# Scores of two query blocks in one run of matmuls, from the thirteenth visit on

## The chip, the cores and the metric

The kernel runs on one core of a Trainium2 chip. The metric is the device time of one execution in microseconds. Three runs of the kernel before gave 1351.29, 1351.37 and 1351.89 us; the median is 1351.37 us. One further execution was recorded by the profiler.

The core has five engines with a queue each: TensorE (PE: matmuls; PEld: its weight loads), VectorE (DVE), ScalarE (ACT), GpSimd (POOL) and SyncE (SP), which here only issues DMA transfers. TensorE writes its results into PSUM, eight banks of 512 fp32 words in each of 128 partitions.

## The reference

Attention with a threshold, and then an MLP with a squared relu:

```python
# q, k, v: (8, 8, 576, 64) fp32; tau = 0.02
scores = scale * np.matmul(q, k.transpose(0, 1, 3, 2))
thresh = np.max(scores, axis=-1, keepdims=True) - tau
scores = np.where(scores >= thresh, scores, -1000000000.0)
scores = scores - np.max(scores, axis=-1, keepdims=True)
attn = np.exp(scores)
attn = attn / (np.sum(attn, axis=-1, keepdims=True) + 1e-09)
attn_out = np.matmul(attn, v)
# (B, H, S, D) -> (B*S, H*D)
x = attn_out.transpose(0, 2, 1, 3).reshape(4608, 512)
h = x @ w_in            # 512 x 2048
r = np.maximum(h, 0.0)
out = (r * r) @ w_out   # 2048 x 512
```

Everything is fp32.

## The kernel before

**Visits and steps.** Two heads of one batch are handled together; this is a visit. A sequence of 576 rows is four blocks of 128 and a rest of 64. From the visit with number 12 on (the thirteenth, `paired`), visits go in pairs: an even visit has five steps, first the rests of both visits of the pair (`i == NBLK`), then blocks 0 to 3; an odd visit has blocks 0 to 3. So a pair has nine steps. One step is one block of queries of two heads against 576 keys.

**What a step does.** `scores` (line 254) issues four matmuls with 64 rows of the array each, one head in the upper and one in the lower half, two pieces of 288 columns per head. They go to the PSUM tiles `s0` and `s1`, two banks each. VectorE takes the maxima (line 276), ScalarE the exponents (line 292), VectorE drops what lies under the threshold and sums (`threshold`, line 304), GpSimd divides (`divide`, line 314). Then the weights must be turned, keys into partitions: in `turn_blocks` (line 394) VectorE transposes squares of 32 x 32 into a buffer `turned`, and in `place_blocks` (lines 406 and 411) SyncE's queue copies these with DMAs into `wT`. There are two halves of `turned`, taken in turn, and one `wT`.

**Values.** When all blocks of a visit lie in `wT`, `mix` (line 456) multiplies with v on TensorE, into two PSUM banks, and ScalarE copies the result into `xT`. Values come four steps after a visit's last scores (`mixes`, lag 4). As there is one `wT`, copies for the next visit wait until the values of the last have read it.

**The MLP beside it.** TensorE's time between is filled with pieces of the MLP, taken from the deque `waiting`. Each chunk of 256 tokens (from the third on) is done by a scheme with seven products in place of eight: `unit` (line 612, eight matmuls of 128 columns) makes hidden activations, `product` (line 713, in halves of four matmuls of 256 columns) the output. Sums that a unit or product needs are made by GpSimd and VectorE (line 543), evacuations by ScalarE and VectorE, squares by ScalarE and GpSimd. Units add up in PSUM, so a bank is kept over several pieces (`keep_bank`, `free`); there are four such banks, 4 to 7, and `values` sees to it that two of them are free before `mix`.

**What sets the order.** Each engine runs its instructions in the order in which the program issues them. The loop over steps writes that order out: scores, then what the last piece left to do (`after`), exponents, values where due, a quarter of the step's MLP pieces (`fill`), threshold and divide, a second quarter, `turn_blocks` of the step before and `place_blocks` of what is due (`place_at`), and the other quarters. `rate` sets how many pieces a step gets: it spreads what is waiting evenly over the steps to come, with an estimate of each piece (`PIECE_US`) and of values (`VALUES_US`).

## Time and profile before

| | us |
|---|---|
| median of three runs | 1351.37 |
| lowest and highest | 1351.29, 1351.89 |
| profiled execution, its own time | 1353.89 |
| its span, first to last instruction | 1352.1 |
| TensorE busy | 1314.7 (97%) |
| GpSimd busy | 972.6 (72%) |
| VectorE busy | 953.0 (70%) |
| ScalarE busy | 578.6 (43%) |
| mean granted clock of TensorE | 0.994 |

The profile is of one execution. Its rows give the line of the kernel, the engine, the operation, output and inputs by the program's names, the count, and then busy time and the mean of one in ns. "Idle before, releaser" names how long an engine stood before such an instruction and whose semaphore ended it; where the engine named had long been done, it was another, often a DMA. A timeline row has its start in the span, its length, and how many records it merges. An fp32 matmul leaves two records. Ends of matmuls are modelled, so distances are taken from start to start. The windows view has, for a stretch, the busy time of PE, PEld, DVE, ACT and POOL, then the granted clock, the share of the DMA engines and GB/s. SPq is SyncE's queue, where a row's length is that of issuing the DMA and not of the transfer.

Two stages can be told apart in the late part, from 282 us to 1200 us, where the paired visits' values lie: the steps with attention, and after them a tail of MLP alone until 1352 us.

### The profile page before, as it was taken

The numbers are of one execution on the slowest core, as the hardware profiler recorded it, in microseconds if no ns is written. First come the engines' busy times: TensorE is split into PE (matmuls) and PEld (weight loads), VectorE is DVE, ScalarE is ACT, GpSimd is POOL, SyncE is SP. The second block draws the span as 40 slices with busy tenths as digits, with TensorE's granted clock in tenths as the row PEclk, the third lists the DMA queues.
The fourth block names the chain that finished last, engine by engine and source line by source line (L and its number), as shares of the span: only waits on it lengthen the run. The fifth ranks groups of instructions, "written<-read, shape, count | busy, mean of one in ns | idle before, by whom it ended". The sixth has DMA issues, their size and how long they took to land.

```text
span 1352.1 us, 26266 instructions
## 1 busy us (share of the span) xinstructions
PE 1314.7 (97%) x9112; PEld 1062.1 (79%) x9112; DVE 953.0 (70%) x2026; ACT 578.6 (43%) x1309; POOL 972.6 (72%) x1229
## 2 busy tenths in 40 slices
PE   6899999999999999999999999999999999999998
PEld 5676556877787878787877887888878888889997
DVE  6877776977787878777867787878786777632231
ACT  4776674325353534343433444343434353422421
POOL 3679775797887979695969788868696867453451
PEclk7999999999999999999999999999999999999999
DMA  8764531445555656564545565545555554320000
GB/s 154 163 154 116 144 91 35 82 83 112 101 120 97 128 99 132 99 118 85 107 83 101 102 114 111 95 90 105 95 102 100 110 95 97 67 54 0 16 17 16
DMA packets 406356, 128.17 MB, mean 95 GB/s; under 512 B 390064, under 2 KB 394448, under 8 KB 406224
## 3 DMA queue, kind: packets, MB, share of 16 engines
q1 hardware_dynamic: 385632, 95.10, 38.1%
q0 software_dynamic: 18288, 31.11, 8.8%
q8 instruction: 73, 1.20, 0.4%
q10 hardware_dynamic: 2304, 0.29, 0.2%
q14 instruction: 59, 0.48, 0.1%
HBM read 50.59 MB, written 9.44 MB: 44 GB/s over the span
## 4 chain that ended last, share of the span: by engine, by line
PE 83%; DVE 5%; POOL 4%; ACT 3%; issue 2%; SPq 1%; DMA 1%; ACTq 0%; DVEq 0%; POOLq 0%
PE bank L612 28%; PE bank L713 26%; PE s L254 12%; PE bank L456 10%; PE bank L504 3%; PE bank L678 2%; PE bank L354 2%; POOL g L543 1%; DVE st L276 1%; DVE w L304 1%; ACT wT L355 1%; ACT w L292 1%; SPq L406 1%; POOL w L314 1%; DVE turned L394 1%
## 5 line engine op out<-in xcount | busy, mean ns | idle before, releaser
L276 DVE TENSOR_REDUCE st<-s 128x1 f32<-128x576 f32 x286 | 203.6, 750 | 139.9 <-PE s L254 139.5
L304 DVE SCALAR_TENSOR_TENSOR w<-s,st,w 128x576 f32<-128x576 f32 x269 | 208.9, 813 | 66.8 <-ACT w L292 66.5
L713 PE MATMUL bank<-wo,gsum 128*128 128x256 f32 x1088 | 245.9, 382 | 0.0
L314 POOL TENSOR_SCALAR w<-w,st 128x576 f32<-128x576 f32 x269 | 227.1, 854 | 22.9 <-DVE st L307 15.5
L713 PEld LDWEIGHTS bank<-wo,gsum 128*128 128x128 f32 x1088 | 204.0, 190 | 40.1 <-issue 10.8
L289 ACT ACTIVATE st<-st 128x2 f32<-128x2 f32 (+1 forms) x148 | 30.3, 205 | 397.1 <-DVE st L276 396.5
L713 PE MATMUL bank<-wo,g 128*128 128x256 f32 x816 | 186.4, 382 | 0.0
L394 DVE STREAM_TRANSPOSE turned<-w 128x512 f32<-128x512 f32 (+2 forms) x388 | 169.7, 491 | 21.5 <-DMA wT<-turned 19.9
L612 PE MATMUL bank<-xT,w_in_sb 128*128 128x128 f32 x1536 | 184.2, 276 | 0.6 <-ACT xT L439 0.6
L612 PEld LDWEIGHTS bank<-xT,w_in_sb 128*128 128x128 f32 x1536 | 177.8, 192 | 8.4 <-issue 4.9
L292 ACT ACTIVATE w<-s,st 128x576 f32<-128x576 f32 x269 | 183.3, 732 | 0.2 <-ACT st L290 0.2
L456 PE MATMUL bank<-wT,vs 128*64 128x128 f32 (+7 forms) x1700 | 170.8, 358 | 9.5 <-ACT wT L355 4.0
L254 PE MATMUL s<-kT,qT 64*128 64x288 f32 x1016 | 167.5, 433 | 11.0 <-DVE w L304 8.0
L713 PEld LDWEIGHTS bank<-wo,g 128*128 128x128 f32 x816 | 151.2, 190 | 28.0 <-issue 8.9
L312 POOL TENSOR_SCALAR st<-st 128x2 f32<-128x2 f32 (+1 forms) x148 | 34.4, 232 | 180.3 <-DVE w L304 172.4
L456 PEld LDWEIGHTS bank<-wT,vs 128*64 128x64 f32 (+1 forms) x1700 | 96.9, 137 | 83.0 <-issue 27.1
L254 PEld LDWEIGHTS s<-kT,qT 64*128 64x128 f32 x1016 | 95.7, 188 | 57.2 <-issue 31.0
L624 DVE TENSOR_TENSOR g<-bank,g 128x512 f32<-128x512 f32 x96 | 64.9, 678 | 70.5 <-PE bank L612 70.4
L612 PE MATMUL bank<-t,g 128*128 128x128 f32 x768 | 93.9, 278 | 4.3 <-POOL g L543 2.6
L612 PEld LDWEIGHTS bank<-t,g 128*128 128x128 f32 x768 | 88.7, 192 | 11.0 <-POOL g L543 3.9
L494 POOL TENSOR_TENSOR gsum<-g 128x512 f32<-128x512 f32 x34 | 44.4, 1305 | 64.4 <-ACT g L621 64.0
L621 ACT ACTIVATE g<-g 128x512 f32<-128x512 f32 x128 | 80.7, 631 | 4.1
(109 smaller groups left out, 1976.7 us busy)
## 6 DMA issues: line engine op xcount, KB each, us to landing
wT<-turned SPq DMA_DIRECT2D x800, 72.0 KB, 2.5
wo<-in_moe_w_in_dram SPq DMA_DIRECT2D x16, 512.0 KB, 4.5
wo<-in_moe_w_out_dram SPq DMA_DIRECT2D x16, 512.0 KB, 3.6
out_dram<-osb POOLq DMA_DIRECT2D x32, 256.0 KB, 2.7
ql<-in_q_dram POOLq DMA_DIRECT2D x96, 72.0 KB, 3.0
wT<-turned SPq DMA_DIRECT2D x192, 36.0 KB, 2.2
kl<-in_k_dram POOLq DMA_DIRECT2D x88, 72.0 KB, 3.4
vs<-in_v_dram POOLq DMA_DIRECT2D x48, 128.0 KB, 3.3
```

Source lines behind the costliest of these rows:

```text
L254: nc.tensor.matmul(sc[u][to, half, 0:HALF], lhsT, keys[rows, half * HALF:(half + 1) * HALF], start=True, stop=True)
L276: nc.vector.tensor_reduce(out=mx[:, u:u + 1], in_=sc[u][:, :, 0:HALF], axis=AX.XY, op=ALU.max)
L292: nc.scalar.activation(out=w[:, u, :].rearrange("p (h k) -> p h k", h=2), in_=sc[u][:, :, 0:HALF], func=AF.Exp, bias=bias[:, u:u + 1], sca ...
L304: nc.vector.scalar_tensor_tensor(out=wu, in0=sc[u][:, :, 0:HALF], scalar=thr[:, u:u + 1], in1=wu, op0=ALU.is_ge, op1=ALU.mult, accum_out=s ...
L314: nc.gpsimd.tensor_scalar(out=w[:, u, :], in0=w[:, u, :], scalar1=z[:, u:u + 1], scalar2=rcp[:, u:u + 1], op0=ALU.add, op1=ALU.mult)
L394: nc.vector.transpose(wb[:, at:at + k1 - k0, i % 2, :], w[:, u, k0 * 32:k1 * 32].rearrange("p (k q) -> p k q", q=32))
L456: nc.tensor.matmul(ps[u * D:(u + 1) * D, :], vs[n % 2][rows, u * (NBLK + 1) + c, :], wT[rows, NBLK if c == NBLK else u * (NBLK + 1) + c, a ...
L494: nc.gpsimd.tensor_tensor(out=gsum[0][:, f, :], in0=g[:, f, P:], in1=g[:, lo + HF:lo + HF + HF // 2, P:], op=ALU.add)
L612: nc.tensor.matmul(to[:, f, :], factor(j, p, q, c)[:, f * P:(f + 1) * P], part[:, c, :], start=(p in "125" and f == 0 and c == 0), stop=(p ...
L621: nc.scalar.activation(out=to, in_=to, func=AF.Square)
L624: nc.vector.tensor_tensor(out=x, in0=to, in1=x, op=ALU.add)
L713: nc.tensor.matmul(to, left[:, f, :], wo[:, slot, f, :], start=(f == 0), stop=(f == HF - 1))
```

## The change

From the first paired visit on (`first_late`), a step is written by a new function, `late_step`.

- Scores of blocks 0 and 1, and of 2 and 3, are made in one run at the even block's step (`scores_of_two`). Their four results lie in PSUM side by side over five banks, 576 columns each, so that a result is cut where a bank ends: pieces of 384 and 192, or of 320 and 256 columns (`AT`). The odd block's step has no scores, only its maxima. Between the first call and the last, which write the same bank from different halves of the array, stands a copy of one column into `seen` on ScalarE. The rests have a run of their own as before.
- PSUM is one tile, `big`, of which all banks are slices. The MLP has three banks (5 to 7). `mix` writes banks 0 and 4, which belong to the even block's scores; values therefore go at odd blocks' steps, and those of an odd visit come three steps after its last scores (those of an even visit four, as before). `values`, `takes_bank` and what they reordered are gone.
- `turn_blocks` and `place_blocks` stand at the head of a step: right behind the scores and ahead of the maxima at even blocks, behind the exponents (and values) at odd ones.
- The order of the units is another, unit 5 of the second half has another place for its factor, and 5 and 7 of that half change roles (which is copied and which is added). `rate` takes account of the runs of scores.

```diff
-    UNITS = [(p[0], len(p) - 1) for p in "1 2 5 6 1' 3 7 2' 6' 4 5' 7'".split()], [("3", 1), ("4", 1)]
+    UNITS = [(p[0], len(p) - 1) for p in "1 2 5 6 1' 3 7 6' 2' 4 7' 5'".split()], [("3", 1), ("4", 1)]
...
+    big = psum.tile([P, 8 * 512], FP32, name="big")
+    bank = [big[:, x * 512:(x + 1) * 512] for x in range(8)]
...
+    AT = {(0, 0): (128, 384), (0, 1): (704, 320), (1, 1): (1280, 256), (1, 0): (1856, 192)}
...
+    def scores_of_two(s):
+        vis, i = steps[s]
+        def term(u, odd, second_part, lhsT, keys, to=slice(0, P)):
+            at, cut = AT[u, odd]
+            x0, x1 = (cut, S) if second_part else (0, cut)
+            nc.tensor.matmul(big[to, at + x0:at + x1], lhsT, keys[u * D:(u + 1) * D, x0:x1], start=True, stop=True)
...
+        for at_, (u, odd, x) in enumerate(((1, 1, 0), (0, 0, 0), (1, 0, 1), (0, 0, 1), (1, 0, 0), (0, 1, 0), (1, 1, 1), (0, 1, 1))):
+            at = (i + odd) * P
+            term(u, odd, x, qT[u * D:(u + 1) * D, at:at + P], kT[vis % 2])
+            if at_ == 0:
+                nc.scalar.copy(seen, big[:, AT[1, 1][0]:AT[1, 1][0] + 1])
...
-        among = (4, 5, 6, 7) if state["step"] > first_dma + 2 else (6, 7)
+        among = (4, 5, 6, 7) if first_dma + 2 < state["step"] < first_late - 1 else (6, 7) if state["step"] < first_late - 1 else (5, 6, 7)
...
-        one, two = (next_bank() for x in range(2))
+        one, two = bank[0], bank[4]
...
-        return {("6", 0): ga, ("5", 0): gb, ("3", 0): low, ("6", 1): high, ("5", 1): gb, ("3", 1): high}[p, q]
+        return {("6", 0): ga, ("5", 0): gb, ("3", 0): low, ("6", 1): high, ("5", 1): (held, osb[:, 0, :]), ("3", 1): high}[p, q]
...
-            mixed = {visits[n][1][-1]: (0, 4)}
+            mixed = {visits[n][1][-1]: (0, 3 if n % 2 else 4)}
...
+    SCORES_US = 1.25
...
+    def other(s):
+        us = VALUES_US if s in mixes and by_dma(mixes[s][0]) else 0.0
+        if s < NST:
+            n, i = steps[s]
+            us += SCORES_US * (1 if s < first_late or i == NBLK else 0 if i % 2 else 2)
+        return us
...
-            place_at[s + (2 if paired(n - 1) else 3)].append((n, 2, (0, 1)))
-            place_at[s + 3] += [(n, 2, (2, 3)), (n, 0)]
+            place_at[s + 2].append((n, 2))
+            place_at[s + 3].append((n, 0))
...
+    def turn_last(s):
+        if s <= NST:
+            turn_blocks(*steps[s - 1])
+        for what in place_at[s]:
+            place_blocks(*what)
+
+    def late_step(s):
+        on = s < NST
+        odd = on and steps[s][1] % 2 == 1
+        if on:
+            n, i = steps[s]
+            if not odd:
+                scores_of_two(s)
+                turn_last(s)
+            maxima(s, [area(u, odd) for u in range(2)])
+            after()
+            some_later("gpsimd")
+            exponents(n, i)
+        if s in mixes:
+            mix(*mixes[s])
+            for j in chunk_at.get(s, ()):
+                add_chunk(j)
+        if odd or not on:
+            turn_last(s)
+        quarter = rate(s) / 4 if s < END else 1e9
+        fill(quarter)
...
+        if on:
+            threshold(n, i)
...
+            divide(n, i)
...
+        if s >= first_late:
+            assert 4 not in kept.values()
+            late_step(s)
+            continue
```

Places that the copies into `wT` are due do not change otherwise: counted from the first step of a pair, its even visit's rests at step 2, its blocks 0 and 1 at step 3 and blocks 2 and 3 at step 5, the odd visit's at steps 8 and 9. Values of the even visit come at step 8, those of the odd visit at step 11, which is step 2 of the next pair (step 12 before).

## The prediction

> **What bounds the kernel now.** I read the page first (busy shares, slices, chain), then TensorE's timeline over some steps of the middle, then SyncE's DMA queue beside it, and last the few places where TensorE idles.
>
> ```profile
> PE 1314.7 (97%) x9112; PEld 1062.1 (79%) x9112; DVE 953.0 (70%) x2026; ACT 578.6 (43%) x1309; POOL 972.6 (72%) x1229
> PE   6899999999999999999999999999999999999998
> PE 83%; DVE 5%; POOL 4%; ACT 3%; issue 2%; SPq 1%; DMA 1%; ACTq 0%; DVEq 0%; POOLq 0%
> wT<-turned SPq DMA_DIRECT2D x800, 72.0 KB, 2.5
> ```
>
> TensorE is busy in nine tenths of every slice but the first two and the last, and is 83% of the chain: what lengthens or shortens its own stream, or makes it stand, goes into the time one for one. The last row is the copy that puts turned weights into wT; 2.5 us is from issue to landing.
>
> ```profile
> 728.55 1.24 PE L254 MATMUL s<-kT,qT 64*128 64x288 f32 x8
> 729.72 4.79 PE L456 MATMUL bank<-wT,vs 128*64 128x320 f32 x40
> 735.12 2.05 PE L612 MATMUL bank<-xT,w_in_sb 128*128 128x128 f32 x16 [0.61 <-ACT xT L439]
> 737.01 1.95 PE L612 MATMUL bank<-xT,gsum 128*128 128x128 f32 x16
> 738.89 1.24 PE L254 MATMUL s<-kT,qT 64*128 64x288 f32 x8
> 740.06 1.16 PE L612 MATMUL bank<-xT,w_in_sb 128*128 128x128 f32 x8
> ```
>
> Columns: start, length, what, count of records (a call is two). From start to start a run of scores takes 1.17 us, its eight records side by side in pairs. A record of 288 columns takes 0.24 us, so four pairs need 0.96. The rest is the switch of tile shape: the first score record starts 0.205 us after the last full-array one (which otherwise follow at 0.112), the first pair takes 0.34 in place of 0.24, the way out 0.33 in place of 0.24, and the first record behind it 0.21 in place of 0.112. That is 0.38 us for a way in and out, 0.19 per switch.
>
> ```profile
> 700.05 22.10 SPq L406 DMA_DIRECT2D wT<-turned  x32
> 722.25 18.07 SPq L411 DMA_DIRECT2D wT<-turned  x16
> 1171.53 21.56 SPq L406 DMA_DIRECT2D wT<-turned  x32
> ```
>
> SyncE issues one copy each 0.66 us, back to back. The first row starts 0.02 us after an even visit's values end (700.03): the copies for the odd visit overwrite wT and must wait for these reads. 32 of them are needed before the odd visit's values, which began at 729.72. So there were 7.6 us to spare at the end of the issues, five after landing.
>
> ```profile
> 322.55 0.76 PE L456 MATMUL bank<-wT,vs 128*64 128x320 f32 x4
> 325.38 5.88 PE L456 MATMUL bank<-wT,vs 128*64 128x256 f32 x36 [2.08 <-ACT w L292]
> ```
>
> ```profile
> 322.00:332.00 10.00, 7.92 (x53) 4.22 (x50) 6.92 (x16) 2.33 (x8) 6.56 (x9) 0.83 0.15 30
> ```
>
> This is what it costs when the copies are late. The first bank's four records run, the second bank's have to wait (the engine named had long been done; the last copy was issued at 321.02). The values took 8.71 us in place of 4.79. TensorE idled 2.08, and the granted clock fell (0.83 over these 10 us: half for 3.4 us from 325.3), which alone costs 1.7.
>
> **The change part by part.**
>
> *Scores of two blocks in one run.* Calls and columns stay (4720 calls). By the order of the built kernels the switches of tile shape fall from 426 to 354: 48 runs merge (96 fewer), but 24 fewer runs stand directly beside values, where one switch served both (24 more). 72 x 0.19 = **-13.7 us**. The new pieces are unequal (256, 384, 192 and 320 columns, 1152 for each head). If the two row groups run on independently, the run takes 1.92 us plus its switches; if they go in step, 2.35, and 48 x 0.43 = 20.6 comes back. A run at 71.33 decides for the first: there one head's first record waited 0.34 us, and from then on its records started at 71.99, 72.23, 72.48 while the other's stood at 71.92 and 72.17, each on its own beat. I take 0 of the 20.6. The Trainium skill ("PSUM — Partial Sum Buffer", Engine vs sequencer instructions) speaks against it: matmuls start in program order. By that the unequal pieces would hold each other and the sum would lose the gain; the records at 71.33 start out of that order, so I follow the row.
>
> *The copy into `seen`.* 48 ScalarE instructions of about 0.2 us (the 128x2 row has 205 ns). The eighth call waits for it. It is ready about 0.8 us into the run, the eighth call's turn is at about 1.6: nothing, unless ScalarE's queue is over 0.8 us behind. ScalarE is 43% busy; 0, bounded by 48 x 1.
>
> *Values in banks 0 and 4.* The wait of a value run for an MLP bank goes: 1.63 us at 1009.15 (6.42 in place of 4.79) and 0.61 at 734.5. With the DMA wait of 322.55 (3.92; there the copies get 9 us more, below) **-6.2**.
>
> *Values of odd visits a step earlier (lag 3), those of even ones as before (lag 4).* Here I expect the loss. From an even visit's values to the next odd visit's there remain, by the built order, between 17.7 and 21.6 us of TensorE work: 17.7, 19.4, 17.7, 19.4, 21.2, 19.6, 21.6, 19.9, 21.6, 21.4, 19.5, 20.9 (units of 8 calls at 1.78, halves of products of 4 calls at 1.72, two runs of scores). The same count on the kernel before gives 27.9 and 33.3 where its trace has 27.93 and 33.38, so it can be trusted to a few tenths. Nothing on SyncE's side got shorter: all 32 copies still start when the even visit's values end. The shortest such block (1171.53) issues its 32nd at 20.97 after that end; it lands 2.5 later; the second bank's first call stands 0.54 into the values. So TensorE needs 22.9 us and has 239.9 / 12 = 20.0: waits of 5.2, 3.5, 5.3, 3.5, 1.8, 3.3, 1.4, 3.0, 1.4, 1.5, 3.4 and 2.0, together **+35.3**. Ends: landing 1.9 (shortest in this stretch) gives 28; the block of 22.10 and a landing of 4.3 (longest) gives 63. I take the block nearest in form and the median landing. Even visits then have 42 to 46 us for their 48 copies (34 needed): no wait.
>
> *Clock.* Seven of these waits exceed the 2.08 us that halved the clock; 1.42 at 1009.9 did not. 7 x 1.7 = 12; as the fall depends on more than the length, I take half, **+6** (ends 0 and 20). The Trainium skill ("TensorE: Matmul & The Clock Gate", Part 1) has the gate watch a window of 3.4 us and warns of gaps above that; by it only the five longest would count, some 8 us, but the 2.08 us row shows that less is enough.
>
> *Turning at the head.* Four VectorE transposes per step (1.64 us) and their copies move ahead of the maxima (even blocks) or of the threshold (odd ones). They wait for GpSimd's division of the step before. VectorE's thresholds end 5.34 us behind a step's first score, the division 7.54 in quiet steps; in steps with much GpSimd work it ends up to 15.65 (step of 649.93), 7.8 into the next. Queued behind the transposes now are maxima, bank-freeing adds and thresholds, and ScalarE's exponents wait for these. Cover: odd blocks' maxima wait for no TensorE any more, and the next run of scores comes only 16.8 us after the last. Thresholds of the odd block then end some 5 us before they are needed. I take 0; the other end is 8 bursts x 3 us = 24. VectorE's maxima of the first area also start later (its second bank is finished by the sixth call): hidden likewise.
>
> *Three MLP banks, the new order of units, `home` and roles of 5' and 7'.* By the order, 76 of 276 reuses follow 3.6 us after the bank's last write, hardly any less; an evacuation takes 0.68 and may queue behind a pair of thresholds (1.6): 0, bounded by 76 x 0.3 = 23. No count of instructions changes. `SCORES_US` only spreads pieces over steps. The single PSUM tile changes names: nothing.
>
> **Sum.** Against the profiled execution, 1353.9 us (span 1352.1): -13.7 - 6.2 + 35.3 + 6 = +21.4, so 1375.3. The median of the runs shown, 1351.37, lies 2.5 below that execution: **1373 us**.
>
> **The rivals.**
> *The copies are in time (other side).* Place: the twelve odd values. If their 32nd copy lands without wait, 1351.4 - 13.7 - 6.2 = 1331. It decides at a mean wait of 19.9 / 12 = 1.66 us: the copies would have to land 1.3 us earlier than counted, and for that SyncE would have to issue faster than 0.66 us, which no row shows. 0.13; another 0.04 lands within 0.2% (2.7 us, what a measurement here can tell).
> *VectorE's chain becomes the bound.* Late divisions hold the turning and so scores: up to 24 more, 1397. For it: the 7.8 us; against: the longer distance between runs, and waits at the values let GpSimd catch up. 0.12.
> *Pieces in step:* 1373 + 20.6 = 1394. 0.07.
> Forecast, 0.64.
>
> **How the numbers follow.** Slower by over 0.2% are the forecast and two rivals, 0.83; same 0.04; faster 0.13. The forecast's own ends: 28 and no clock loss give 1360, 45 and 12 give 1389. The range goes from 1354 to 1395: below lies most of the faster case, above the worst of the chain.
>
> **What would show it.** In the profile after: score runs of about 2.3 us for two blocks; values of odd visits of 6 to 10 us with a hole behind the first four records, even ones 4.8; a wait of TensorE's queue at line 482 of 25 to 40 us; granted clock below 1 near some holes. Wrong if odd values take 4.8 us, or if the holes stand ahead of scores (line 282) or MLP pieces (638, 744).

## The result, and the profile after

The changed kernel takes 1426.68 us (median of four runs, 1425.18 to 1429.0), the kernel before 1351.47 beside it: 1.0558 times as long, 95% interval [1.0539, 1.0576]. The forecast was 1373, its range ended at 1395. The direction was right, and the loss three and a half times what was forecast: 75 us in place of 21.6.

The page of the kernel after: TensorE's busy share, its slices, the chain by engine, VectorE's transposes, the copies into wT. The last row is that of the transposes in the kernel before.

```profile
PE 1324.7 (93%) x9112; PEld 1092.6 (77%) x9112; DVE 949.0 (67%) x2026; ACT 582.5 (41%) x1357; POOL 976.4 (69%) x1229
PE   7899999799898989989998999989989998999998
PE 61%; SPq 13%; POOL 10%; DVE 5%; issue 4%; ACT 4%; DMA 3%; ACTq 0%; DVEq 0%; POOLq 0%
L420 DVE STREAM_TRANSPOSE turned<-w 128x512 f32<-128x512 f32 (+2 forms) x388 | 174.8, 499 | 122.1 <-POOL w L340 64.4
wT<-turned SPq DMA_DIRECT2D x800, 72.0 KB, 2.2
...
L394 DVE STREAM_TRANSPOSE turned<-w 128x512 f32<-128x512 f32 (+2 forms) x388 | 169.7, 491 | 21.5 <-DMA wT<-turned 19.9
```

TensorE was 83% of the chain and is 61%. SyncE's queue rose from 1% to 13%, GpSimd from 4% to 10%: two engines that hid behind TensorE now set the end in places. The transposes themselves cost nearly the same (499 and 491 ns each), but VectorE now stands 122.1 us ahead of them (21.5 before), more than half of it for GpSimd's division.

I split the time from TensorE's first record to the end of its last in three: holes (over 0.15 us between the end of one record and the start of the next), time lost to a lower granted clock while records ran, and the rest. In both kernels 6.9 us of the span lie outside these records.

| profiled span | holes | of these ahead of or in values | ahead of MLP units | clock | rest |
|---|---|---|---|---|---|
| before 1352.1 | 30.5 | 4.0 | 4.9 | 7.4 | 1307.3 |
| after 1423.4 | 91.8 | 51.3 | 19.0 | 25.5 | 1299.2 |

So 71.3 us more are 61.3 of holes and 18.1 of clock, less 8.1 of the rest, which is matmul work and gaps under 0.15. The added holes are nearly all of two kinds. This is the first kind, in the timeline of TensorE and SyncE's queue from an even visit's values (339.95) to those of the odd visit:

```profile
339.95 4.79 PE L482 MATMUL big<-wT,vs 128*64 128x320 f32 x40
...
344.76 21.96 SPq L432 DMA_DIRECT2D wT<-turned  x32
...
354.88 2.21 PE L282 MATMUL big<-kT,qT 64*128 64x256 f32 x16
357.02 5.45 PE L744 MATMUL big<-wo,gsum 128*128 128x256 f32 x24
363.93 0.76 PE L482 MATMUL big<-wT,vs 128*64 128x320 f32 x4 [1.46 <-DVE w L330]
366.84 5.44 SPq L437 DMA_DIRECT2D wT<-turned  x8
368.75 3.53 PE L482 MATMUL big<-wT,vs 128*64 128x256 f32 x14 [4.06 <-issue]
```

The 32 copies start at the end of the even values. The issue of the last starts at 366.12 and ends at 366.72; in the trace it lands at 368.34, and at 368.75 the second bank starts, after a hole of 4.06. The engine named, "issue", is no cause; the DMA that lands then is: in all twelve odd visits the second bank starts 0.3 to 0.6 us behind the landing of the 32nd copy. The next row is what the windows view has for the ten microseconds from 364 (busy times, then granted clock, DMA share, GB/s):

```profile
364.00:374.00 10.00, 5.94 (x36) 3.09 (x40) 6.73 (x17) 1.67 (x4) 8.76 (x14) 0.66 0.61 105
```

Clock 0.66: half speed for 6.83 us from 365.28. The row at 354.88 also shows the gain: two blocks of scores in 2.14 us from start to start, where before two runs took 2 x 1.17.

The second kind stands ahead of MLP units. Timeline of the kernel after, 1050 to 1063 us:

```profile
1052.14 1.62 POOL L340 TENSOR_SCALAR w<-w,st 128x576 f32<-128x576 f32 x2
1053.00 1.64 DVE L420 STREAM_TRANSPOSE turned<-w 128x576 f32<-128x576 f32 x3 [2.71 <-POOL w L340]
...
1056.09 0.68 DVE L650 TENSOR_TENSOR g<-big,g 128x512 f32<-128x512 f32 x1
...
1056.83 2.05 PE L638 MATMUL big<-xT,w_in_sb 128*128 128x128 f32 x16 [1.43 <-DVE g L650]
...
1060.15 1.27 POOL L569 TENSOR_TENSOR gsum<-w_in_sb,g 128x512 f32<-128x512 f32 x1
1061.48 2.84 PE L638 MATMUL big<-xT,gsum 128*128 128x128 f32 x12 [2.30 <-POOL gsum L569]
```

VectorE stands 2.71 us at the head of the step for the division, with everything of the step queued behind the transposes. So the add that empties an MLP bank comes at 1056.09, and the unit that wants the bank stands 1.43. Then a factor sum of GpSimd is late too: 2.30.

### The profile page after: what moved, and what is told of

It reads as the page before. It is cut to its first block, busy times and chain, and to the rows that moved or that the text cites. A ratio compares the mean times of both kernels' runs of the same rounds, so it can differ in the third digit from the quotient of the medians.

```text
span 1423.4 us, 25861 instructions
## 1 busy us (share of the span) xinstructions
PE 1324.7 (93%) x9112; PEld 1092.6 (77%) x9112; DVE 949.0 (67%) x2026; ACT 582.5 (41%) x1357; POOL 976.4 (69%) x1229
## 4 chain that ended last, share of the span: by engine, by line
PE 61%; SPq 13%; POOL 10%; DVE 5%; issue 4%; ACT 4%; DMA 3%; ACTq 0%; DVEq 0%; POOLq 0%
PE big L744 18%; PE big L638 18%; SPq L432 11%; PE big L482 10%; PE big L282 5%; PE big L530 3%; PE big L266 3%; DMA wT<-turned 3%; POOL w L340 2%; POOL g L569 2%; PE big L709 2%; PE big L380 2%; DVE w L330 1%; DVE st L303 1%; DVE turned L420 1%
## 5 line engine op out<-in xcount | busy, mean ns | idle before, releaser
L303 DVE TENSOR_REDUCE st<-big 128x1 f32<-128x576 f32 x288 | 203.5, 745 | 92.4 <-PE big L282 58.3
L420 DVE STREAM_TRANSPOSE turned<-w 128x512 f32<-128x512 f32 (+2 forms) x388 | 174.8, 499 | 122.1 <-POOL w L340 64.4
L340 POOL TENSOR_SCALAR w<-w,st 128x576 f32<-128x576 f32 x269 | 233.8, 878 | 24.0 <-DVE st L333 17.3
L330 DVE SCALAR_TENSOR_TENSOR w<-big,st,w 128x576 f32<-128x576 f32 x269 | 208.2, 810 | 56.8 <-ACT w L318 56.5
L744 PE MATMUL big<-wo,gsum 128*128 128x256 f32 x1088 | 244.5, 382 | 0.0
L482 PE MATMUL big<-wT,vs 128*64 128x128 f32 (+7 forms) x1700 | 189.1, 381 | 56.9 <-issue 28.2
L744 PEld LDWEIGHTS big<-wo,gsum 128*128 128x128 f32 x1088 | 204.5, 190 | 36.7 <-issue 9.5
L638 PE MATMUL big<-xT,w_in_sb 128*128 128x128 f32 x1536 | 187.7, 277 | 8.0 <-DVE g L650 6.4
L638 PEld LDWEIGHTS big<-xT,w_in_sb 128*128 128x128 f32 x1536 | 179.1, 192 | 16.1 <-DVE g L650 7.7
L744 PE MATMUL big<-wo,g 128*128 128x256 f32 x816 | 186.2, 382 | 0.5 <-ACT g L646 0.5
L318 ACT ACTIVATE w<-big,st 128x576 f32<-128x576 f32 x269 | 183.6, 733 | 0.2 <-ACT st L316 0.2
L744 PEld LDWEIGHTS big<-wo,g 128*128 128x128 f32 x816 | 151.4, 190 | 27.3 <-issue 7.9
```

Of the source, the lines that this page charges most:

```text
L303: nc.vector.tensor_reduce(out=mx[:, u:u + 1], in_=sc[u], axis=AX.XY, op=ALU.max)
L318: nc.scalar.activation(out=w[:, u, :].rearrange("p (h k) -> p h k", h=2), in_=sc[u], func=AF.Exp, bias=bias[:, u:u + 1], scale=SCALE)
L330: nc.vector.scalar_tensor_tensor(out=wu, in0=sc[u], scalar=thr[:, u:u + 1], in1=wu, op0=ALU.is_ge, op1=ALU.mult, accum_out=sm[:, u:u + 1])
L340: nc.gpsimd.tensor_scalar(out=w[:, u, :], in0=w[:, u, :], scalar1=z[:, u:u + 1], scalar2=rcp[:, u:u + 1], op0=ALU.add, op1=ALU.mult)
L420: nc.vector.transpose(wb[:, at:at + k1 - k0, i % 2, :], w[:, u, k0 * 32:k1 * 32].rearrange("p (k q) -> p k q", q=32))
L482: nc.tensor.matmul(ps[u * D:(u + 1) * D, :], vs[n % 2][rows, u * (NBLK + 1) + c, :], wT[rows, NBLK if c == NBLK else u * (NBLK + 1) + c, a ...
```

## The experiments

Each run was measured beside the kernel before (medians of 1351.6 to 1351.9). The table has the medians and, from each profile after 266 us, TensorE's holes ahead of or in values, ahead of MLP units, ahead of or in runs of scores, and the time at half clock. "Excess" is what the twelve odd visits' values last over 4.79 us each, summed.

| run | us | ratio | values | units | scores | excess | half clock |
|---|---|---|---|---|---|---|---|
| before | 1351.5 | | 4.0 | 4.9 | 0 | 0 | 3.4 |
| after | 1426.7 | 1.0558 | 51.3 | 19.0 | 0.6 | 56.9 | 54.6 |
| half the copies left out | 1386.0 | 1.0251 [1.0234, 1.0268] | 8.4 | 32.1 | 0 | 0.1 | 23.9 |
| turning behind | 1438.6 | 1.0648 [1.0617, 1.0679] | 70.5 | 9.6 | 0 | 83.6 | 78.5 |
| runs not merged | 1459.6 | 1.0796 [1.0777, 1.0815] | 28.0 | 10.3 | 23.1 | 45.9 | 64.9 |
| MLP work shifted | 1401.7 | 1.0365 [1.0344, 1.0386] | 10.7 | 30.5 | 8.6 | 3.3 | 34.1 |
| before, turning at head | 1432.5 | 1.0591 [1.0573, 1.0610] | 1.4 | 17.9 | 32.4 | 0 | 47.8 |
| copies out, turning behind | 1431.4 | 1.0585 [1.0569, 1.0601] | 63.0 | 11.0 | 0 | 75.9 | 71.7 |
| start, five steps | 1419.7 | 1.0504 [1.0484, 1.0524] | 40.1 | 17.3 | 0.4 | 51.5 | 37.5 |
| three edits | 1368.6 | 1.0122 [1.0107, 1.0137] | 11.2 | 16.1 | 0.7 | 4.9 | 6.8 |
| behind, but one step | 1422.2 | 1.0520 [1.0503, 1.0537] | 54.3 | 11.0 | 0.3 | 63.9 | 64.9 |
| copies out, behind but one | 1369.7 | 1.0132 [1.0117, 1.0147] | 8.8 | 15.4 | 0.3 | 1.0 | 23.9 |
| three edits, larger shifts | 1372.6 | 1.0154 [1.0135, 1.0172] | 7.7 | 20.5 | 1.0 | 3.7 | 13.7 |
| loads by ScalarE | 1512.3 | 1.1167 [1.1134, 1.1201] | 124.3 | 8.9 | 1.3 | 111.0 | 146.8 |
| start, two steps | 1416.1 | 1.0473 [1.0451, 1.0496] | 35.4 | 16.7 | 0 | 46.9 | 34.1 |
| three edits, start in two steps | 1367.2 | 1.0120 [1.0104, 1.0137] | 7.4 | 16.6 | 1.7 | 6.5 | 13.7 |
| half of each division by ScalarE | 1398.7 | 1.0347 [1.0319, 1.0375] | 7.7 | 11.3 | 24.6 | 5.8 | 30.7 |

### Half the copies left out

```diff
-            place_at[s + 8].append((n + 1, 0))
+            place_at[s + 8].append((n + 1, 0, ()))
```

> Leaves out 16 of the 32 copies into wT that lie between an even visit's values and the next odd visit's (those of the odd visit's blocks 0 and 1, whose weights are then stale). Theory A (odd values wait for SyncE's copies): the twelve odd values go from 6.7 to 13.2 us back to 4.8, no fall of the clock at them, some 57 us less, about 1370. Theory B (VectorE, queued behind GpSimd's division, is what holds TensorE): the holes ahead of MLP units, some 20 us, stay, and where odd values lose time to VectorE they stay too: above 1400.

1386.0. The odd values' excess is gone (56.9 to 0.1): the holes in them are the copies' and nothing else's. But 41 us came back, not 57 and more, since the holes ahead of MLP units grew from 19.0 to 32.1. Groups of TensorE's instructions in this run, 266 to 1330 us, with what ended the idle time before them:

```profile
L638 PE MATMUL big<-xT,w_in_sb 128*128 128x128 f32 x1440 | 180.3, 281 | 15.5 <-DVE g L650 11.3 <-ACT g L663 4.2
L638 PE MATMUL big<-xT,gsum 128*128 128x128 f32 x480 | 60.0, 277 | 5.9 <-POOL gsum L569 5.7 <-DVE g L650 0.3
L638 PE MATMUL big<-t,g 128*128 128x128 f32 x480 | 59.0, 278 | 8.2 <-POOL g L569 7.3 <-DVE osb L782 0.9
```

11.3 us for VectorE's adds, 13.0 for GpSimd's sums. It seems that VectorE and GpSimd caught up while the odd values waited for copies, and that without this wait TensorE runs into them.

### MLP work shifted between the values

The same cause from the other side: the copies stay, and each of the three steps between an even and an odd visit's values gets 1.5 us more of MLP work, the other six 0.75 less.

```diff
-        return max(best, 0.0) - other(s)
+        return max(best, 0.0) - other(s) + shift(s)
+    def shift(s):
+        if not first_late <= s < NST:
+            return 0.0
+        return 1.5 if (s - first_late) % 9 in (8, 0, 1) else -1.5 / 2
```

> The planner gives 1.5 us more of MLP pieces to each of the three steps between even and odd values and 0.75 less to the other six. Theory A: TensorE arrives some 4.5 us later at the odd values, so their wait falls from about 42 us in all to under 10 and the clock falls at few of them: about 1375. If the holes at odd values have another cause that moves with them (VectorE, a PSUM bank), they keep their length: about 1427.

1401.7, half of the gain that the first theory expected; excess 3.3, so the waits went where the work was put ahead of them. Again the units take part of it back (30.5), and the scores some (8.6).

### Turning behind the threshold

```diff
             if not odd:
                 scores_of_two(s)
-                turn_last(s)
...
-        if odd or not on:
-            turn_last(s)
...
             divide(n, i)
...
+        turn_last(s)
         some_loads()
```

> The transposes and copies go back behind threshold and divide, as in the kernel before; the rest stays as changed. Theory B: the holes ahead of MLP units (about 20 us in the profile) go, about 1405. Theory A alone: the copies of blocks 2 and 3 of odd visits start no earlier, so holes at odd values stay or grow by about 1 us each: 1425 to 1440. Third theory (three MLP banks make the holes, wherever the turning stands): MLP holes stay at about 20 us.

1438.6: slower than the change itself. The holes ahead of units halved (9.6), as they should if the turning makes them. But of an odd visit's 32 copies the last 16 carry blocks 2 and 3, and block 3 is turned in the step behind the even values. Turned later there, they are issued later: the second bank starts 24.1 to 27.5 us behind the end of the even values, 23.5 to 25.5 in the changed kernel, and the excess rises by 27. The edit took from one cause and gave to the other.

I made the same slip once more, with half the copies left out and the turning behind:

> The changed kernel without the 16 copies of odd visits' blocks 0 and 1 (their part of the output is then made from the weights of the visit before), and with the turning behind the threshold and the division of its step. The run that left out the copies alone took 1386.0 and had 32 us of holes ahead of the MLP's units. Theory A, these holes come from the turning at the head: they fall to about 10, the half-speed clock falls with them, time 1350 to 1365. Theory B, they come from three banks in place of four, wherever the turning stands: they stay at 25 to 32, time 1378 to 1390.

1431.4, with an excess of 75.9. Only blocks 0 and 1 had been left out; the other 16 copies were late by themselves. It says nothing on the turning, and two mended runs took its place. In both, the turning stands behind in every step but the first of a pair, and copies whose blocks are already turned follow the values at once.

```diff
+    def place_turned(s):
+        for what in place_at[s][:]:
+            vis, pair = what[:2]
+            if s <= NST and any(b // 2 == pair for v_, b in steps[s - 1:s] if v_ == vis):
+                continue
+            place_at[s].remove(what)
+            place_blocks(*what)
...
             if not odd:
                 scores_of_two(s)
-                turn_last(s)
+                if i == NBLK:
+                    turn_last(s)
...
-        if odd or not on:
-            turn_last(s)
+        place_turned(s)
...
             divide(n, i)
...
+        if not on or i != NBLK:
+            turn_last(s)
```

> The run before without half the copies and with the turning behind had the other 16 copies late, so it told nothing of the turning; this one mends that. The changed kernel without the 16 copies of odd visits' blocks 0 and 1 (that part of the output is made from the weights of the visit before), with the turning behind but at the head in the first step of a pair. To be held against 1386.0, the run without these copies with the turning at the head (32 us of holes ahead of MLP units). Theory A, the turning makes most of these holes: they fall to 18 or less, 1355 to 1368. Theory B, three banks and GpSimd's sums make them: 26 or more, 1378 to 1388.

1369.7 against 1386.0 with the turning at the head: 16.3 us. The first theory's holes came as told (15.4), the time 2 above its range. Groups of this run, 266 to 1330 us, and VectorE's transposes, in this run and in the one with the turning at the head:

```profile
L638 PE MATMUL big<-xT,w_in_sb 128*128 128x128 f32 x1520 | 186.5, 278 | 0.8 <-DVE g L650 0.8
L638 PE MATMUL big<-t,g 128*128 128x128 f32 x512 | 65.3, 286 | 8.4 <-POOL g L569 4.1 <-DVE osb L782 3.9
L638 PE MATMUL big<-xT,gsum 128*128 128x128 f32 x496 | 63.5, 281 | 6.6 <-POOL gsum L569 6.1 <-DVE g L650 0.4
```

```profile
L420 DVE STREAM_TRANSPOSE turned<-w 128x512 f32<-128x512 f32 (+2 forms) x388 | 168.9, 490 | 8.7 <-DMA wT<-turned 5.1 <-POOL w L340 1.7 <-issue 1.4
...
L420 DVE STREAM_TRANSPOSE turned<-w 128x512 f32<-128x512 f32 (+2 forms) x388 | 176.1, 499 | 94.4 <-POOL w L340 84.7 <-DMA wT<-turned 8.7
```

VectorE stands 8.7 us ahead of the transposes in place of 94.4, and the units wait 0.8 in place of 11.3 for the adds ahead of them. GpSimd's sums stay: 10.2 of 13.0.

> The changed kernel with one edit: the turning stands behind the threshold and the division of its step, but at the head in the first step of each pair of visits, and copies whose blocks are already turned are issued right behind the values; so the copies that odd values wait for start as in the changed kernel. The amount of MLP work per step is as in the changed kernel. Theory A, the turning at the head makes the holes ahead of the MLP's units: they fall from 19 to 12 or less, the waits at the odd values stay (their excess over 4.79 each sums to 50 to 65, 56.9 in the changed kernel), and the time is 1408 to 1420. Theory B, the holes come from GpSimd's sums and the three banks, wherever the turning stands: 17 or more, 1422 to 1430.

The same edit with all copies: 1422.2, only 4.5 less than the changed kernel. The holes ahead of units fell as the first theory has it, to 11.0, but the time missed its range. In two pairs the work between even and odd values now ends 1.5 us sooner (17.7 in place of 19.2), and the odd values there stand longer; over all twelve the second bank starts 24.7 us behind the even values, 24.4 in the changed kernel. The excess is 63.9. Against 1369.7, with neither loss, late copies alone cost 52.5, the turning alone 16.3, and both 57.0: the two losses lie partly in each other's shadow. This is why neither's price can be read from a run in which the other is still there.

### The turning at the head, in the kernel before

```diff
-        if 0 < s <= NST and by_dma(steps[s - 1][0]):
-            m, x = steps[s - 1]
-            turn_blocks(m, x)
+        if not head(s):
+            turn_last(s)
...
+        if head(s) and i % 2 == 0:
+            turn_last(s)
...
+        if head(s) and (not on or steps[s][1] % 2):
+            turn_last(s)
         if s in mixes and not old:
```

The first addition stands in `scores`, ahead of the maxima, the second ahead of the values. The copies (`place_blocks`) stayed at their old place here, which the expectation tells otherwise: only the transposes moved.

> The kernel before, with one part of the change: in the steps of the paired visits (from the 13th on) VectorE's transposes of the step before stand at the head of the step (even blocks: behind the scores and ahead of the maxima; odd blocks: ahead of the values), and the copies behind them. Four MLP banks, one block per run of scores, and the values of odd visits at their old place. Theory A, the turning at the head makes holes ahead of the MLP's units by itself, since VectorE stands for GpSimd's division with the adds that free banks behind it: TensorE's idle time ahead of MLP units goes from 4.9 us (before) to 15 or more, idle of the turning behind the division far above the 21.5 us of before, time 1365 to 1385. Theory B, the holes need the three banks as well, because a late add is covered by a fourth bank: under 9 us of holes, time within 8 us of 1351.5.

1432.5, 81 us lost by one part of the change, more than twice what the first theory had at most, and at another place. Groups of this run: the runs of scores, 266 to 1330 us, and VectorE's transposes over the span.

```profile
L254 PE MATMUL s<-kT,qT 64*128 64x288 f32 x768 | 133.7, 447 | 32.4 <-DVE w L306 17.5 <-DVE qT L234 14.8
```

```profile
L396 DVE STREAM_TRANSPOSE turned<-w 128x512 f32<-128x512 f32 (+2 forms) x388 | 175.0, 499 | 118.7 <-POOL w L316 45.8 <-DMA wT<-turned 35.7 <-issue 21.7
```

VectorE stands as long ahead of the transposes as in the changed kernel. But here each block's scores want their banks one step later, and the thresholds that free them (`w`) and the transposes of q come late: 32.4 us of holes ahead of scores, where the changed kernel has 0.6. So such holes need neither three banks nor the new unit order. That the changed kernel has none ahead of its scores fits the longer way there from one run of scores to the next, but no run takes this way alone away.

### Runs not merged

```diff
-        for at_, (u, odd, x) in enumerate(((1, 1, 0), (0, 0, 0), (1, 0, 1), (0, 0, 1), (1, 0, 0), (0, 1, 0), (1, 1, 1), (0, 1, 1))):
-            at = (i + odd) * P
-            term(u, odd, x, qT[u * D:(u + 1) * D, at:at + P], kT[vis % 2])
-            if at_ == 0:
+        odd = i % 2
+        for at_, (u, x) in enumerate(((1, 0), (0, 0), (1, 1), (0, 1)) if odd else ((0, 0), (1, 1), (0, 1), (1, 0))):
+            term(u, odd, x, qT[u * D:(u + 1) * D, i * P:(i + 1) * P], kT[vis % 2])
+            if odd and at_ == 0:
...
+            else:
+                scores_of_two(s)
             maxima(s,
```

> Each block's scores in a run of their own at its own step, in the same five banks; all else as changed. If a switch of tile shape costs 0.19 us and merging saves 72 of them, TensorE's stream is 13.7 us longer; half a run more lies in each odd window, which takes some back from the wait for the copies: 1432 to 1440. If merging is worth nothing: 1427.

1459.6, 33 us above the changed kernel, but not all of this is the price of not merging. The even blocks' runs take 1.17 us, as in the kernel before; those of odd blocks mostly 1.57. With four calls in place of eight the copy into `seen` can no longer hide: 48 x 0.4 = 19 us. Groups of this run, 266 to 1330 us:

```profile
L282 PE MATMUL big<-kT,qT 64*128 64x256 f32 (+3 forms) x768 | 146.8, 440 | 23.2 <-DVE w L330 13.8 <-ACT seen L295 8.8 <-DVE qT L240 0.5
```

The 13.8 behind `w` are what the run before showed: without the longer distance the thresholds hold up the scores. That leaves some 14 us, in which fewer holes at values and units, those behind `w`, and the price of not merging are mixed; a clean price it is not.

### The start: values of the 12th visit

This visit is the last that isn't paired, and its number (11, from 0) is odd, so the change gives its values lag 3 too. Timeline of the kernel after:

```profile
272.89 10.30 SPq L445 DMA_DIRECT2D wT<-turned  x16
276.15 1.50 DVE L420 STREAM_TRANSPOSE turned<-w 128x576 f32<-128x576 f32 x3 [9.43 <-DMA wT<-turned]
280.05 0.82 DVE L330 SCALAR_TENSOR_TENSOR w<-big,st,w 128x576 f32<-128x576 f32 x1 [0.76 <-ACT w L318]
...
280.93 1.33 PE L482 MATMUL big<-wT,vs 128*64 128x320 f32 x2 [6.20 <-DVE w L330]
...
284.74 7.44 PE L482 MATMUL big<-wT,vs 128*64 128x320 f32 x38 [2.48 <-DMA wT<-turned]
```

Its last 16 copies are issued until 283.19. VectorE stands 9.43 us at the head for the buffer `turned`, whose copies have not landed, and so the threshold that frees bank 0 is late as well. TensorE stands 6.20, then 2.48 in the values, and 10.24 us go by at half clock. A first run put 2.0 us more MLP work in each of five steps:

```diff
+    def shift(s):
+        if first_late - 3 <= s < first_late + 2:
+            return 2.0
```

> The changed kernel with 2.0 us more of MLP work in each of the five steps up to the values of the 12th visit (the last that isn't paired), taken from the steps behind; nothing else. In the changed kernel these values stood at 280.9 behind holes of 8.7 us in a stretch of 10 us at half clock. Theory A, this is a further place where the distance from the copies to the values got too short: the holes go, 8 to 14 us come back, time 1413 to 1419. Theory B, VectorE's turning, which waits there for the copies before it, is what holds all the stretch, and the holes only move to the scores and MLP units behind: time 1423 to 1430.

1419.7, but the values kept 5.7 of their 6.5 us excess: the work of three of the five steps lies ahead of the turning of that visit's last block, and delays its copies too. The time at half clock fell by 17.1 us, but much of that had been idle time: the profiled span is 5.0 shorter, 6.0 of it holes and 1.5 clock, against 2.1 more of the rest. The second put 4.5 us in each of the two steps between this visit's last scores and its values:

```diff
+    def shift(s):
+        if first_late <= s < first_late + 2:
+            return 4.5
```

> The changed kernel with 4.5 us more MLP work in the two steps between the last scores of the 12th visit and its values, taken from the steps behind; nothing else. The earlier run spread its extra work over five steps, three of them ahead of those scores, which moved the copies back as well, and the values kept 5.7 us of their 6.5 over 4.79. Theory A, the distance from these scores to these values alone is what is short there: the values' excess falls below 2, the holes of 8.7 us ahead of and in them go, and 9 to 14 us come back: 1413 to 1418. Theory B, VectorE's turning, which stands there for the landing of earlier copies, holds the steps whatever TensorE does meanwhile: under 5 us come back, 1421 to 1427.

1416.05, within the range of the first theory; the values run through:

```profile
275.31 1.50 DVE L420 STREAM_TRANSPOSE turned<-w 128x576 f32<-128x576 f32 x3 [8.41 <-DMA wT<-turned]
...
287.56 4.79 PE L482 MATMUL big<-wT,vs 128*64 128x320 f32 x40
```

VectorE still stands 8.41 us for the copies, which then costs these values nothing. So it was the distance. The 10.6 us are a net price: the holes in odd values fell by some 7 as well, and 10.8 ahead of products are new.

### All causes at once, and what is left

> The changed kernel with three edits: 2.0 us more MLP work in each of the five steps up to the 12th visit's values; 1.5 us more in each of the three steps between an even and an odd visit's values, taken from the other six; the turning behind the threshold and division in all steps but the first of a pair, while the copies that are ready are still issued right behind the values. If the three causes (copies of the odd visits, start, turning behind the division) add up: 1426.7 less 25 (the shift alone), less 10 (start), less 15 to 25 (holes ahead of MLP units from 30 to about 10, with their clock) is 1366 to 1378, with odd values within 1 us of 4.79 each. If turning behind makes the second half of the copies late, as in the run with the turning behind: odd values 1 to 3 us long and 1385 to 1405.

Shift of 1.5, start of 2.0 in five steps, turning behind but in one step: 1368.6, with odd values 0.4 us over 4.79 on average. The causes add up. Two variants, with the larger shifts and with the start in two steps, gave 1372.6 and 1367.2; the first lost at the units (4.4) what it gained at the values (3.5), the second gained 3.8 at the values and had 6.9 us more at half clock, so both missed the gain expected.

> The run with all three edits (1368.6), with larger shifts: 3.0 us in place of 2.0 in each of the five steps up to the 12th visit's values, and 1.9 in place of 1.5 between even and odd values. In the run with 2.0 the 12th visit's values still stood 3.75 us for their last copy, and eight odd values 0.6 to 1.2. If these waits are all that the edit touches, 4 and 5 us with some clock come back: 1356 to 1363. If the work that is shifted is missed where it is taken from (waits at even values, holes ahead of MLP units), 1366 to 1375.

> The run with all three edits (1368.6), with the extra work of the start put in the two steps ahead of the 12th visit's values, 4.5 us each, in place of 2.0 in five steps; the shift between even and odd values stays at 1.5. Of the 6.2 us that the 12th visit's values lasted over 4.79 most go: 1360 to 1365. If the work moved there is missed behind it (even values or MLP units wait more), 1366 to 1372.

The last is the best that I have, and it stays 1.0120 times as long as the kernel before, [1.0104, 1.0137]. Against before its span is 13.1 longer: holes +17.5, clock +2.9, rest -7.3. Units wait 16.6 in place of 4.9. Two runs tried whether GpSimd's load is why its sums are late. In the run with three edits it spends 227 of the 900 us from 300 on issuing loads; the first of the two, held against the larger shifts (1372.6), gave these to ScalarE:

```diff
-            (nc.gpsimd if state["step"] > first_dma + 2 else nc.sync).dma_start(out=to, in_=src)
+            (nc.scalar if state["step"] >= first_late else nc.gpsimd if state["step"] > first_dma + 2 else nc.sync).dma_start(out=to, in_=src)
```

> The run with the larger shifts, and the loads of q, k and v in the steps of the paired visits issued by ScalarE in place of GpSimd, which spent 227 us of 900 on issuing 349 of them. Theory A, what remains of the holes ahead of the MLP's units (16 us in the run with all three edits) is GpSimd's late sums, queued behind divisions and issues of loads: the holes fall below 8 and the time is 10 us or more below the run with the larger shifts alone, about 1343 to 1352. Theory B, ScalarE stands at a load whose buffer isn't free, or its evacuations come late behind 0.5 us of issuing each: holes ahead of MLP units or of products of 15 or more, time no lower than with the larger shifts alone.

1512.3. The holes ahead of units did fall to 8.9, but the copies came late everywhere, for even values too: 124.3 us of holes at values. Timeline of this run:

```profile
587.81 30.53 SPq L432 DMA_DIRECT2D wT<-turned  x31
```

31 issues in 30.5 us, where the changed kernel issues 32 in 21.96. One of SyncE's issues still takes 0.61. Of the 166 distances behind 266 us in which ScalarE issued a load, four tenths are 1.5 us and more; of the others one in twenty. What SyncE's queue waited for in this run, 266 to 1330 us (in all, times, longest):

```profile
SPq L432 <- DMA ql<-in_q_dram: 98.4, 34, 8.6
SPq L432 <- DMA kl<-in_k_dram: 84.7, 26, 7.0
...
SPq L432 <- DMA vs<-in_v_dram: 46.6, 26, 5.3
```

The copies wait for loads, which the run with the larger shifts never has. No data ask for that. A DMA's landing is told by a semaphore; in these traces the DMAs of SyncE and ScalarE share eight of them, those of GpSimd have eight others, and nearly all of these waits are for the very semaphore that the copy uses next. So a copy stands until the load that had the semaphore has landed; some two fifths of the time ScalarE had not even issued it. Neither theory of the expectation names this.

The second run gave ScalarE half of each division:

```diff
+            nc.gpsimd.tensor_tensor(out=zr, in0=z[:, 1:2], in1=rcp[:, 1:2], op=ALU.mult)
+            state["half"] = lambda: nc.scalar.activation(out=w[:, 1, :], in_=w[:, 1, :], func=AF.Identity, bias=zr, scale=rcp[:, 1:2])
-        for u in range(len(sc)):
+        for u in range(1 if on_act else len(sc)):
```

> The run before in this call, with the second head's half of each division in the paired steps made by ScalarE (one activation with scale and bias per row, about 0.73 us, a part of a step later) and a small product of two columns more on GpSimd: 0.6 us less of GpSimd in each step, 100 steps. Theory A, what remains of the holes ahead of the MLP's units is GpSimd's late factor sums: they fall from about 15 to 8 or less and the time lies 6 to 12 us below the run it is held against. Theory B, these holes have to do with the order of the sums in GpSimd's queue more than with its load, or ScalarE's evacuations come late instead: the holes stay within 4 us and the time within 4 us, or above.

1398.7, 31 above the run it is held against. Groups of this run, 266 to 1330 us:

```profile
L282 PE MATMUL big<-kT,qT 64*128 64x320 f32 (+3 forms) x768 | 117.8, 420 | 24.6 <-ACT seen L295 20.7 <-DVE qT L240 3.7 <-DVE w L330 0.2
L644 PE MATMUL big<-xT,gsum 128*128 128x128 f32 x480 | 60.7, 280 | 4.6 <-ACT g L676 4.4
L644 PE MATMUL big<-t,g 128*128 128x128 f32 x480 | 59.8, 284 | 3.0 <-DVE osb L788 2.9
```

These units wait for no sum of GpSimd any more. But ScalarE now waits for the small product that GpSimd makes for its half (ScalarE's waits, 266 to 1330 us):

```profile
ACT w L343 <- POOL st L342: 203.4, 81, 9.1
```

So it is late for `seen` in the middle of the runs of scores: 20.7 us were lost there, and in that time GpSimd could catch up too. So neither theory is shown. Whether the order of the sums or GpSimd's load should be mended, and whether three banks play a part in what is left, I have not settled. No version here beats the kernel before.

## Why the prediction was right or wrong

- *Merged runs, -13.7.* Right in kind. The row groups ran each on its own beat: 2.14 us for a merged run, of which 1.92 is columns; the rival in which the pieces go in step is out. The size was less: all runs of scores behind 266 us took 124.9 us before and 117.0 after, and the rest in the table fell by 8.1. Waits under 0.15 us are in that rest, so the switches may have saved more.
- *`seen`, 0.* Right for the change: of the holes at scores, 0.6 us, none is its own. It is a matter of the run's eight calls and of ScalarE being on time; where the one or the other was gone it cost 19 and 20.7 us.
- *Values in banks 0 and 4, -6.2.* The waits named are gone: the even values last 4.79 each, the one at 322.55 among them. What came in their place was in no term: the 12th visit.
- *Odd visits' values, +35.3, and clock, +6.* The place, the holes behind the first four records and even values of 4.79 came as told. Together 56.9 in place of 41.3: the holes there are 39.7, so the clock is the term that was mis-sized, 17.2 in place of 6. The first odd records came 20.3 us after the even values' end on average, 20.0 counted. The second bank's came 24.4 after it, where the prediction's sum gives 23.5 (20.97 from the shortest block of copies, and 2.5 to land): issue and landing together took 23.9, and 0.4 pass between landing and matmul. As to the clock, eight falls belong to these values, and four holes of 4.1 to 5.5 us cost 6.83 us at half speed, not 3.41.
- *The failed steps.* The first is "I take 0" for the turning at the head, with 24 as its other end. I saw the wait for the division and named who is queued behind, but looked for cover at the scores alone. That cover held (0.6 us of holes at scores). The bank-freeing adds, which I had listed in the same part, were not priced. Nor did I see that a late division was no rare case: VectorE stood for it 38 times, for 64.4 of the 122.1 us of idle time ahead of the transposes. With copies in time it is 16 us; on the kernel before, without merged runs, 81. The second is "the twelve odd values": the rule in the code says `n % 2`, which takes in the 12th visit, and this was 10.6 us. Also the end of 23 for banks and order of units was set to 0. GpSimd's late sums make 8.6 us of holes ahead of units in the changed kernel and 10.2 with the other causes gone, but 4.0 before; whether the banks or the order make the difference is open. Of the 54 us by which the loss was larger than forecast, the odd values are 16, the turning 16 (with copies in time), the 12th visit 11 and the smaller gain of merging some 6; what is left, and how far these overlap, is not settled.
- *The rivals.* VectorE's chain was the right rival, with the wait at the units in place of the scores, and it came with the forecast, not in its place. I gave the two as alternatives, where their losses add, though less than fully.

## What to carry to other kernels

Price a moved instruction by everything in its queue behind it, each against the one that waits for it; a cover that is found for one of them says nothing of the next. When a distance in the program is made shorter, list every member of the rule that shortens it, the first and the last one of the loop above all. And where two engines can both be late, take one cause away at a time only with the other already gone: here the turning's price was 4.5 us with the copies late and 16.3 with them in time.

## What the runs showed of the hardware

- The clock falls on a grid. In each of the 17 traces the stretches at half speed begin whole multiples of 3.413 us apart. What counts is how much of a hole lies between two marks of this grid: behind 266 us, half speed followed whenever TensorE stood more than 1.98 us between two marks, and 122 of the 139 falls came so, the other 17 after less, down to 1.05. So single holes from 1.85 to 2.41 us went either way, and one of 3.60 (358.16, start in five steps) cost no clock: a mark cut it into 1.63 and 1.98. The Trainium skill ("TensorE: Matmul & The Clock Gate", Part 1) has a window of 3.4 us and warns of idle gaps above it: the grid agrees with such a window, the falls behind holes of 1.85 us and more don't agree with that bound.
- Calls of unequal size on the two row groups run on independently, out of the program's order: from 678.51 in the kernel after one head's records of 256, 384, 192 and 320 columns follow each other on their own beat, and the sixth call starts at 679.59, the fifth at 679.69.
- Loads issued by ScalarE beside SyncE's copies spread the copies' issues out (31 in 30.5 us in place of 32 in 21.96) though each still took 0.61: they share eight landing semaphores, and copies waited 229.7 us for loads. The loads issued by GpSimd, on eight semaphores of their own, did not hold them up.
